# An attention and expert kernel on one core: scores begun half a step sooner, and all ten pairs of query chunks sharing their weights

## The chip, the core and the metric

The kernel runs on one NeuronCore of a Trainium2 chip. PE is the matrix engine (PEld are its weight loads), DVE the vector engine, ACT the scalar engine, POOL the general engine and SP the engine whose queue issues nearly all transfers. The time is the device time of one execution in microseconds (us); lower is better.

## The reference

Two layers one after the other, in fp32: an attention without softmax over 8 sequences of 2496 tokens, and a layer of 8 experts of which each token takes at most one.

```python
scale = 1.0 / S                                  # S = 2496, z: (8, 2496, 64)
scores = scale * np.matmul(z, z.transpose(0, 2, 1))
attn = np.maximum(scores, 0.0) ** 2
x = u * np.matmul(attn, v)                       # u, v: (8, 2496, 256)
x = x.reshape(19968, 256)
do_compute = x @ w_skip > 0
xc = x[do_compute]
e_idx = np.argmax(xc @ w_gate, axis=1)           # and gate_w, its softmax probability
for e in range(8):                               # w1[e]: 256x1024, w2[e]: 1024x256
    h = np.maximum(xc[e_idx == e] @ w1[e], 0.0)
    out[e_idx == e] = xc[e_idx == e] + gate_w[e_idx == e, None] * (h @ w2[e])
```

Queries and keys are the same array z, so the matrix of scores is symmetric, and so are the weights `attn`.

## The kernel before

**Chunks and steps.** A sequence (a batch `b`) is cut into five chunks of queries, c = 0 to 4: four of 512 and the last of 448. A chunk is worked off in ten steps, p = 0 to 9, of 256 keys each; the keys of step p belong to chunk j = p // 2. `ORDER[c]` says in which order chunk c takes its ten steps. There are 8 x 5 x 10 = 400 steps in `steps`. What is called step k below is the place in that order, 0 to 9.

**A step.** `scores` (L280): six matmuls of 64 rows into a PSUM tile `ps` (two buffers). `weights`: ACT makes `r` = relu (L323) and squares it (L324); `r` has five buffers. fp32 is carried as a pair of rounded values: `high` rounds `r` to `ah` (L346, on ACT where `on_act` says so, otherwise on DVE), `low` has DVE make `al` = `r` - `ah` (L350). `ah` and `al` have three buffers each. `attend` (L377): 24 matmuls of 64 rows into the accumulators `acc`, in two halves of 12, d = 0 and d = 1 (the two halves of the features); the step of the last keys has 18. The second half of a chunk's first step is put off into its second, and that of its last but one into its last. A step's scores are issued `LA` = 2 steps ahead: in step k, `stage(s + LA)` issues the scores of step k + 2 on PE, then relu, square, `ah` and `al` are queued on ACT and DVE, and then the 24 matmuls of step k follow.

**Shared weights.** For a pair of chunks (c, j) in `PAIRS`, c < j, the weights that chunk c computes for the keys of chunk j are those that chunk j needs for the keys of chunk c, transposed. `keep` (L297) has DVE turn `r` into a tile `rt` (two buffers, one for a pair of chunks, two transposes a step); two steps later `put_some` issues four transfers `kept<-rt` of 256 KB, in runs of 512 bytes. `ahead` calls `recall` (L311) five steps before the step: one transfer `r<-kept` of 512 KB into a buffer of `r`. A recalled step has no scores, relu or square; in chunk 4 its `ah` and `al` are made in three pieces each. The first batch does not share the pairs of chunk 0. The turning of a chunk's last but one step waits in `put_off`.

**A chunk's end** (`finish`): ACT copies a half of the sums out of PSUM (L405), DVE adds the other (L407), then multiplies by `u` (`mul`, L410), turns the rows (L414), and SP stores them twice (L423) at the ends of steps 3 and 4 of the next chunk. After every second chunk the routing of its tokens follows (`gates`, L445, on PE; small DVE operations L478 to L534). SP's queue is in program order: a transfer that waits for its data or its buffer holds back all behind it. From 1230 us on the experts' part runs (`unit`, L639 to L662).

Of the kernel before, what the change touches and what calls it, by code (L numbers as in the profile page):

```python
# [27 lines left out]

PAIRS = ((0, 1), (0, 2), (0, 3), (1, 2), (1, 3), (2, 3), (2, 4), (3, 4))
ORDER = (
# [22 lines left out]
def attn_moe(ctx, tc, zT, uT, v, wg, w1, w2, cst, pad, out):  # L55
# [183 lines left out]
    def on_act(ci, p):  # L239
        b, c = ci // NQ, ci % NQ  # L240
        j = p // 2
        if (b, c) == (0, 0):
            return p in (4, 6)
        return (j, c) in pairs(b) or (c, j) in pairs(b) or p in EXTRA[c]
# [69 lines left out]
    put_off = []  # L314
# [393 lines left out]
    NP = NB // 2  # L708
    steps = [(ci, p) for ci in range(len(chunks)) for p in order(ci // NQ, ci % NQ)]
    LA = 2  # L710
    NC = len(chunks)
    NZ = SZ // QC
    todo = {}
    aa = {}
# [3 lines left out]

        todo.setdefault(s // 2, []).append(f)

    old, known = {}, set()

    def stage(s):
        if s < len(steps):
            aa[s], high, low = weights(*steps[s], old.pop(s, None), s % NP == NP - 2)
            return high, low
        return lambda: None, lambda: None

    def put_some():

# [5 lines left out]
    def ahead(s):  # L736
        if s < len(steps):
            ci, p = steps[s]
            if (p // 2, ci % NQ) in pairs(ci // NQ):
                old[s] = recall(ci, p)  # L740
                known.add(s)


    def later(s, k, load, *args):
# [5 lines left out]
    for ci, (b, q0, n) in enumerate(chunks):  # L750
# [3 lines left out]
            if chunks[ci + 1][2] == QC:  # L754
                at(s0 + 10, lambda ci=ci: straight(ci + 1))
        if ci == 0:
            first = [(4 * j - 8, j % 2, 3, load_z, j) for j in range(2, NZ)]
            first += [(2 * g - 4, 1, 4, load_v, g) for g in range(2, NB // 2)]
            for s1, _, k, load, j in sorted(first, key=lambda x: x[:2]):
                eng = nc.vector  # L760
                if s1 - k < 0:
                    at(s1, load(0, j, eng))
                else:
                    later(s1 - k, k, load, 0, j, eng)
            at(14, lay_pads)
# [31 lines left out]
    ctx.enter_context(tc.manual_schedule(engines=set(ENGINES)))  # L797

    for s in range(LA):
        for f in stage(s):  # L800
            f()
    accs = {}
    new, left = [], []
    for s, (ci, p) in enumerate(steps):
        b, q0, n = chunks[ci]
        k = s % NP
# [3 lines left out]
            accs[ci] = [[ps_acc.tile([P, QC], F32, name="acc", tag="acc") for _ in range(2)] for _ in range(2)]  # L810
        acc = accs[ci]
        if k < NP - 1:
            high, low = stage(s + LA)
            if k < NP - 2 or s + LA in known:
                high()
                low()
                high = low = lambda: None
            while k == NP - 3 and put_off:
                put_off.pop()()
            attend(b, n, p, 0, acc[0], *aa[s], k == 0, False)  # L820
            for t in () if k in (0, NP - 2) else (s - 1, s) if k == 1 else (s,):
                attend(b, n, steps[t][1], 1, acc[1], *aa.pop(t), t % NP == 0, False)
            rest = high, low
        else:


            part, mul, rows0, rows1, store = finish(ci)
            attend(b, n, p, 0, acc[0], *aa[s], False, True)

            high, low = rest  # L830
            if s + 1 < len(steps) and not on_act(*steps[s + 1]):
                high()
                low()
                high = low = lambda: None
            part(0, 1, acc[0])
            part(0, 0, acc[0])
            high()
            low()
            high, low = stage(s + LA)
            attend(b, n, steps[s - 1][1], 1, acc[1], *aa.pop(s - 1), False, False)  # L840
            if s + LA in known:

                high()
                low()
                high = low = lambda: None
            attend(b, n, p, 1, acc[1], *aa.pop(s), False, True)
            part(1, 1, acc[1])
            high()
            part(1, 0, acc[1])
            low()  # L850
            mul()
            accs.pop(ci)

            new.append(ci)
# [222 lines left out]
```

## Time and profile before

| | before |
|---|---|
| time, median of 3 runs | 1719.31 us (1716.77 to 1723.87) |
| the profiled execution | 1723.13 us, of which 1721.3 us from the first to the last instruction |
| granted clock of PE | 0.996 of full speed over the span |
| PE busy | 98% of the span |
| DVE, ACT, POOL busy | 69%, 67%, 30% |
| moved by DMA | 267 MB |

A busy share is an average over the attention part (about 1230 us) and the experts' part (about 490 us), which have different limits; the chunks of one batch are told apart further down.

### The profile page before, as it was taken

The numbers are of one execution on the slowest core, as the hardware profiler recorded it, in microseconds if no ns is written. First come the engines' busy times: TensorE is split into PE (matmuls) and PEld (weight loads), VectorE is DVE, ScalarE is ACT, GpSimd is POOL, SyncE is SP. The second block draws the span as 40 slices with busy tenths as digits, with TensorE's granted clock in tenths as the row PEclk, the third lists the DMA queues.
The fourth block names the chain that finished last, engine by engine and source line by source line (L and its number), as shares of the span: only waits on it lengthen the run. The fifth ranks groups of instructions, "written<-read, shape, count | busy, mean of one in ns | idle before, by whom it ended". The sixth has DMA issues, their size and how long they took to land.

```text
span 1721.3 us, 39714 instructions
## 1 busy us (share of the span) xinstructions
PE 1679.4 (98%) x15690; PEld 1519.3 (88%) x15690; DVE 1191.2 (69%) x2108; ACT 1151.4 (67%) x1494; POOL 522.7 (30%) x545
## 2 busy tenths in 40 slices
PE   9999999999999999999999999999989999999998
PEld 7889888888988898898889888888889999999998
DVE  7878888887887788788788878877653333333433
ACT  8888887887888888788888877878433323323321
POOL 1103212311320221131123123122344567546631
PEclk9999999999999999999999999999999999999999
DMA  5575688477758847875784787568452244224210
GB/s 197 129 187 156 159 240 229 95 211 226 171 148 215 241 101 200 242 183 145 197 233 112 210 243 192 131 180 219 117 129 64 83 106 113 72 69 108 85 42 31
DMA packets 397964, 267.34 MB, mean 155 GB/s; under 512 B 199920, under 2 KB 328305, under 8 KB 397648
## 3 DMA queue, kind: packets, MB, share of 16 engines
q1 hardware_dynamic: 383584, 240.45, 52.2%
q0 software_dynamic: 13632, 22.99, 4.7%
q8 instruction: 138, 2.26, 0.5%
q14 instruction: 178, 1.46, 0.3%
q10 hardware_dynamic: 432, 0.18, 0.0%
HBM read 145.80 MB, written 118.06 MB: 153 GB/s over the span
## 4 chain that ended last, share of the span: by engine, by line
PE 79%; DVE 6%; ACT 6%; issue 4%; DMA 4%; SPq 0%; POOL 0%; DVEq 0%; ACTq 0%; POOLq 0%
PE acc L377 46%; PE y L662 12%; PE psh L639 11%; PE ps L280 8%; DVE al L350 3%; DMA out<-o,idt 2%; ACT ah L346 2%; ACT r L323 2%; ACT r L324 1%; PE psm L445 1%; DVE rt L297 1%; PE pst L604 1%; DMA kept<-rt 1%; DVE ah L346 1%; DMA r<-kept 0%
## 5 line engine op out<-in xcount | busy, mean ns | idle before, releaser
L377 PE MATMUL acc<-ah,vh 64*128 64x512 f32 (+1 forms) x3120 | 626.6, 373 | 6.1 <-ACT ah L346 3.7
L377 PE MATMUL acc<-ah,vl 64*128 64x512 f32 (+1 forms) x3120 | 611.0, 371 | 0.1
L350 DVE TENSOR_TENSOR al<-r,ah 128x1024 fp32r<-128x1024 f32 (+3 forms) x464 | 488.0, 1068 | 157.3 <-ACT ah L346 132.1
L377 PE MATMUL acc<-al,vh 64*128 64x512 f32 (+1 forms) x3120 | 484.2, 374 | 10.0 <-DVE al L350 8.6
L536 POOL DMA_INDIRECT lst<-pair,dest x160 | 196.5, 1228 | 859.8 <-DVE dest L534 780.7
L377 PEld LDWEIGHTS acc<-ah,vh 64*128 64x128 f32 x3120 | 337.7, 186 | 47.9 <-ACT ah L346 6.7
L323 ACT ACTIVATE r<-ps 128x1024 f32<-128x1024 f32 (+1 forms) x278 | 279.0, 1003 | 146.4 <-PE ps L280 124.6
L377 PEld LDWEIGHTS acc<-ah,vl 64*128 64x128 f32 x3120 | 336.8, 186 | 30.9 <-DVE vl L127 0.5
L377 PEld LDWEIGHTS acc<-al,vh 64*128 64x128 f32 x3120 | 309.0, 186 | 56.2 <-DVE al L350 26.5
L346 ACT CAST ah<-r 128x1024 fp32r<-128x1024 f32 (+3 forms) x381 | 329.2, 889 | 39.4 <-PE acc L377 29.2
L324 ACT ACTIVATE r<-r 128x1024 f32<-128x1024 f32 (+1 forms) x278 | 289.9, 1043 | 8.8
L649 ACT ACTIVATE hh<-psh 128x512 fp32r<-128x512 f32 (+2 forms) x172 | 96.2, 572 | 279.0 <-PE psh L639 200.5
L662 PE MATMUL y<-w2t,hh 128*128 128x256 f32 (+1 forms) x1328 | 233.6, 280 | 2.3 <-ACT hh L649 1.9
L650 DVE SCALAR_TENSOR_TENSOR hl<-psh,hh 128x512 fp32r<-128x512 f32 (+2 forms) x172 | 110.1, 655 | 159.1 <-ACT hh L649 127.2
L662 PEld LDWEIGHTS y<-w2t,hh 128*128 128x128 f32 (+1 forms) x1328 | 204.1, 191 | 4.7 <-ACT hh L649 2.9
L662 PE MATMUL y<-w2t,hl 128*128 128x256 f32 (+1 forms) x664 | 185.1, 279 | 6.3 <-DVE hl L650 3.2
L639 PE MATMUL psh<-xt,w1h 128*128 128x256 f32 (+3 forms) x896 | 176.1, 296 | 1.9 <-issue 1.8
L297 DVE STREAM_TRANSPOSE rt<-r 128x512 f32<-128x512 f32 x244 | 158.3, 687 | 1.7 <-DMA kept<-rt 1.7
L639 PEld LDWEIGHTS psh<-xt,w1h 128*128 128x128 f32 x896 | 140.8, 191 | 4.4 <-issue 2.6
L662 PEld LDWEIGHTS y<-w2t,hl 128*128 128x128 f32 (+1 forms) x664 | 126.8, 191 | 7.9 <-DVE hl L650 4.0
L639 PE MATMUL psh<-xt,w1l 128*128 128x256 f32 (+3 forms) x448 | 132.0, 295 | 1.6 <-issue 1.6
L695 POOL DMA_INDIRECT out<-o,idt x77 | 76.6, 994 | 156.6 <-DVE o L692 123.2
(186 smaller groups left out, 1794.5 us busy)
## 6 DMA issues: line engine op xcount, KB each, us to landing
kept<-rt SPq DMA_DIRECT2D x244, 256.0 KB
r<-kept SPq DMA_DIRECT2D x122, 512.0 KB
raw<-in_v SPq DMA_DIRECT2D x80, 256.0 KB
ut<-in_uT SPq DMA_DIRECT2D x32, 512.0 KB
xr<-xrow SPq DMA_DIRECT2D x128, 128.0 KB
out<-xrow SPq DMA_DIRECT2D x128, 128.0 KB
raw<-in_w SPq DMA_DIRECT2D x64, 256.0 KB
zf<-in_zT SPq DMA_DIRECT2D x40, 256.0 KB
```

Source lines behind the costliest of these rows:

```text
L280: nc.tensor.matmul(to, k[h, o : o + P], queries(ci, q, h, n), start=(m == 0), stop=(m == 2))
L297: nc.vector.transpose(t[:, :, 32 * k : 32 * k + 32].rearrange("p (k a) i -> p a k i", k=4), r[:, x, :].rearrange("p (a k i) -> p a k i", a ...
L323: nc.scalar.activation(r[:, :, :n], ps[:, :, :n], AF.Relu, scale=isc)
L324: nc.scalar.activation(r[:, :, :n], r[:, :, :n], AF.Square)
L346: (nc.scalar.copy if on_act(ci, p) else nc.vector.tensor_copy)(h_, r_)
L350: nc.vector.tensor_sub(l_, r_, f32(h_))
L377: nc.tensor.matmul(acc[t][:, :n], w[h, x, dd], by_halves(a[h, x, :n]), start=(first and t not in halves[:m]), stop=(last and t not in halv ...
L536: put = nc.gpsimd.indirect_dma_start(out=lst, out_offset=bass.IndirectOffsetOnAxis(ap=dest[:, t : t + 1], axis=0), in_=pair[:, t, :], in_o ...
L639: nc.tensor.matmul(ps[:, j * W : (j + 1) * W], wt[:, a, o : o + P], by_halves(x[:, d, :W]) if alt else x[:, d, :W], start=(m == 0), stop=( ...
L649: nc.scalar.activation(oh, by, AF.Relu)
L650: nc.vector.scalar_tensor_tensor(ol, by, 0.0, f32(oh), op0=ALU.max, op1=ALU.subtract)
L662: nc.tensor.matmul(ys[t], h[:, tt], by_halves(w2t[f][:, k, :]), start=(f == 0 and m == 0 and t % share == 0), stop=(f == NF - 1 and m == 2 ...
```

## The change

`PAIRS` becomes all ten pairs (c, j) with c < j, so (0, 4) and (1, 4) are new; the first batch shares six instead of five. Over the 8 batches that is 6 + 7 x 10 = 76 pairs instead of 5 + 7 x 8 = 61, so 30 more steps are recalled, all of them in chunk 4. `ORDER[0]` takes the steps as they come (8 stood between 3 and 4), `ORDER[1]` changes, too. `stage` is split: `begin` issues scores, relu and square, `rounding` queues `ah` and `al`. In step k, `rounding(s + 2)` comes first, then the first half of the step's matmuls, then `begin(s + 3)`, then the second half. The turning of a chunk's last two steps (not only of the last but one) waits in `put_off`, which is now emptied behind the chunk's `mul`. In the first chunk the loads of z are begun two half steps sooner.

```diff
-PAIRS = ((0, 1), (0, 2), (0, 3), (1, 2), (1, 3), (2, 3), (2, 4), (3, 4))
+PAIRS = tuple((i, j) for j in range(5) for i in range(j))
 ORDER = (
-    (0, 1, 2, 3, 8, 4, 5, 6, 7, 9),
-    (2, 3, 0, 4, 1, 5, 8, 6, 7, 9),
+    (0, 1, 2, 3, 4, 5, 6, 7, 8, 9),
+    (2, 3, 0, 4, 5, 1, 6, 7, 8, 9),
     (4, 0, 1, 6, 2, 7, 3, 8, 9, 5),
     (6, 0, 2, 1, 8, 3, 9, 4, 5, 7),
     (0, 1, 2, 3, 4, 5, 6, 7, 8, 9),
...
-    def stage(s):
+    def begin(s):
         if s < len(steps):
-            aa[s], high, low = weights(*steps[s], old.pop(s, None), s % NP == NP - 2)
-            return high, low
-        return lambda: None, lambda: None
+            aa[s], high, low = weights(*steps[s], old.pop(s, None), s % NP >= NP - 2)
+            rounds[s] = high, low
+
+    def rounding(s):
+        for f in rounds.pop(s, ()):
+            f()
...
-            first = [(4 * j - 8, j % 2, 3, load_z, j) for j in range(2, NZ)]
+            first = [(4 * j - 10, j % 2, 3, load_z, j) for j in range(2, NZ)]
...
         if k < NP - 1:
-            high, low = stage(s + LA)
-            if k < NP - 2 or s + LA in known:
-                high()
-                low()
-                high = low = lambda: None
-            while k == NP - 3 and put_off:
-                put_off.pop()()
+            rounding(s + LA)
             attend(b, n, p, 0, acc[0], *aa[s], k == 0, False)
+            if k != 1:
+                begin(s + LA + 1)
             for t in () if k in (0, NP - 2) else (s - 1, s) if k == 1 else (s,):
                 attend(b, n, steps[t][1], 1, acc[1], *aa.pop(t), t % NP == 0, False)
-            rest = high, low
+                if k == 1 and t < s:
+                    begin(s + LA + 1)
         else:
             part, mul, rows0, rows1, store = finish(ci)
             attend(b, n, p, 0, acc[0], *aa[s], False, True)
-            high, low = rest
-            if s + 1 < len(steps) and not on_act(*steps[s + 1]):
-                high()
-                low()
-                high = low = lambda: None
             part(0, 1, acc[0])
             part(0, 0, acc[0])
-            high()
-            low()
-            high, low = stage(s + LA)
             attend(b, n, steps[s - 1][1], 1, acc[1], *aa.pop(s - 1), False, False)
-            if s + LA in known:
-                high()
-                low()
-                high = low = lambda: None
+            rounding(s + LA)
+            begin(s + LA + 1)
             attend(b, n, p, 1, acc[1], *aa.pop(s), False, True)
             part(1, 1, acc[1])
-            high()
             part(1, 0, acc[1])
-            low()
             mul()
+            while put_off:
+                put_off.pop(0)()
             accs.pop(ci)
```

PE's order where two steps of chunk 0 in the middle of the kernel meet, before. `acc_11726` and `acc_11727` take the second half (d = 1) of a step, `acc_11724` and `acc_11725` the first half of the next.

```order
L377 MATMUL acc_11726<-al_11739,vh_10567 128x512
L377 MATMUL acc_11727<-al_11739,vh_10567 128x512
L280 MATMUL ps_11870<-zqh_11551,zh_11289 128x512 x2
L280 MATMUL ps_11870<-zql_11552,zh_11289 128x512 x2
L280 MATMUL ps_11870<-zqh_11551,zl_11290 128x512 x2
L377 MATMUL acc_11724<-ah_11767,vh_10823 128x512
L377 MATMUL acc_11725<-ah_11767,vh_10823 128x512
```

PE's order in the changed kernel at the same place: `acc_11745` and `acc_11746` take the first half of a step, `acc_11747` and `acc_11748` its second.

```order
L377 MATMUL acc_11745<-al_11750,vh_10594 128x512
L377 MATMUL acc_11746<-al_11750,vh_10594 128x512
L280 MATMUL ps_11871<-zqh_11572,zh_11312 128x512 x2
L280 MATMUL ps_11871<-zql_11573,zh_11312 128x512 x2
L280 MATMUL ps_11871<-zqh_11572,zl_11313 128x512 x2
L377 MATMUL acc_11747<-ah_11749,vh_10594 128x512
L377 MATMUL acc_11748<-ah_11749,vh_10594 128x512
```

The six matmuls of the scores have moved from between two steps to between the halves of the step before.

DVE's order at the end of chunk 0, before: the second halves of the sums are added (`xrow`), `al` of a later step, `mul` (`ut`), and the next chunk's first steps.

```order
L407 TENSOR_TENSOR xrow_12173<-acc_11726,xrow_12173 128x512
L350 TENSOR_TENSOR al_12222<-r_12196,ah_12221 128x1024
L410 TENSOR_TENSOR ut_11597<-xrow_12173,ut_11597 128x1024
L534 TENSOR_SCALAR dest_11721<-df_12035 128x2
L350 TENSOR_TENSOR al_12247<-r_12100,ah_12246 128x1024
L350 TENSOR_TENSOR al_12273<-r_12269,ah_12272 128x1024
```

DVE's order in the changed kernel at the same place.

```order
L350 TENSOR_TENSOR al_12225<-r_12197,ah_12224 128x1024
L407 TENSOR_TENSOR xrow_12200<-acc_11747,xrow_12200 128x512
L410 TENSOR_TENSOR ut_11618<-xrow_12200,ut_11618 128x1024
L297 STREAM_TRANSPOSE rt_12240<-r_12035 128x4x4x32 x2
L297 STREAM_TRANSPOSE rt_12240<-r_12106 128x4x4x32 x2
L534 TENSOR_SCALAR dest_11742<-df_12058 128x2
L350 TENSOR_TENSOR al_12263<-r_12123,ah_12262 128x1024
L350 TENSOR_TENSOR al_12289<-r_12285,ah_12288 128x1024
```

Four transposes, those of the new pair (0, 4), stand between `mul` and the next `al`; the `al` ahead of `mul` now stands ahead of the second halves' sum.

SP's order in chunk 3 of a batch in the middle, before. `kept_230` is the pair (3, 4), `kept_229` the pair (2, 4), `raw` a load of v.

```order
L423 DMA xr<-xrow 32x16x64 x4
L423 DMA out<-xrow 32x16x64 x4
L173 DMA ut<-in_uT 128x2x448
L734 DMA kept_230<-rt 32x16x128 x4
L102 DMA raw<-in_v 128x512
L311 DMA r<-kept_229 128x2x512
L110 DMA zf<-in_zT 128x512
```

SP's order in the changed kernel at the same place: `kept_229` is now the pair (0, 4), `kept_230` (1, 4), `kept_231` (2, 4), `kept_232` (3, 4).

```order
L423 DMA xr<-xrow 32x16x64 x4
L423 DMA out<-xrow 32x16x64 x4
L311 DMA r<-kept_229 128x2x512 x2
L173 DMA ut<-in_uT 128x2x448
L739 DMA kept_232<-rt 32x16x128 x4
L311 DMA r<-kept_230 128x2x512 x2
L102 DMA raw<-in_v 128x512
L311 DMA r<-kept_231 128x2x512
L110 DMA zf<-in_zT 128x512
```

Four more recalls, for the first four steps of chunk 4, stand around the write of the pair (3, 4).

## Rows read from the trace of the kernel before

**Rows 1.** The page: the span, and the busy time of each engine with its share of the span.

```profile
span 1721.3 us, 39714 instructions
PE 1679.4 (98%) x15690; PEld 1519.3 (88%) x15690; DVE 1191.2 (69%) x2108; ACT 1151.4 (67%) x1494; POOL 522.7 (30%) x545
```

**Rows 2.** Windows: the five chunks (0 to 4) of the fifth batch, one line each, bounds in us, then length and busy us of each engine, the granted clock, the share of the 16 DMA engines' time, GB/s.

```profile
624.30:655.40 31.10, 31.10 (x291) 27.29 (x289) 25.28 (x32) 28.77 (x29) 10.18 (x12) 1.00 0.55 136
655.40:687.60 32.20, 31.92 (x316) 26.55 (x315) 26.76 (x56) 26.55 (x31) 3.72 (x3) 1.00 0.69 181
687.60:717.50 29.90, 29.38 (x272) 25.75 (x268) 21.70 (x28) 24.28 (x28) 8.27 (x9) 1.00 0.87 243
717.50:749.70 32.20, 31.20 (x306) 26.13 (x308) 26.43 (x52) 22.75 (x28) 5.13 (x4) 1.00 0.80 212
749.70:775.60 25.90, 25.90 (x272) 25.60 (x270) 22.86 (x36) 21.52 (x35) 9.00 (x12) 1.00 0.63 172
```

**Rows 3.** The chain that ended last, in order of time (start us, length us, what). The first two rows stand at the same place of chunk 4 in the third and in the fifth batch; those behind them are a step with 448 queries, one with 512, and the routing's matmuls.

```profile
446.41 12.48 PE acc L377 x132
751.62 12.48 PE acc L377 x132
...
764.72 2.27 PE acc L377 x24
766.99 0.60 PE ps L280 x6
...
818.89 2.59 PE acc L377 x24
821.48 0.65 PE ps L280 x6
845.44 1.01 PE psm L445 x32
```

**Rows 4.** Waits over the whole span: engine and line, what ended the wait, us in total, times, longest us.

```profile
ACT r L323 <- PE ps L280: 124.6, 107, 4.3
DVE al L350 <- ACT ah L346: 132.1, 130, 3.2
PEld acc L377 <- DVE al L350: 26.5, 46, 1.2
PE acc L377 <- DVE al L350: 8.6, 18, 0.8
PEld acc L377 <- ACT ah L346: 6.7, 8, 1.2
```

**Rows 5.** Lines by form: the operations of DVE and then of ACT in a chunk 4 (901.2 to 929.5 us); after the bar busy us, mean ns of one.

```profile
L350 DVE TENSOR_TENSOR al<-r,ah 128x896 fp32r<-128x896 f32 x5 | 5.5, 1092 | 1.1 <-ACT ah L346 0.6
L350 DVE TENSOR_TENSOR al<-r,ah 128x384 fp32r<-128x384 f32 x8 | 4.0, 541 | 0.0
L350 DVE TENSOR_TENSOR al<-r,ah 128x128 fp32r<-128x128 f32 x4 | 1.1, 285 | 0.0
L346 DVE CAST ah<-r 128x896 fp32r<-128x896 f32 x3 | 2.0, 673 | 0.0
...
L324 ACT ACTIVATE r<-r 128x896 f32<-128x896 f32 x4 | 3.8, 952 | 0.1
L323 ACT ACTIVATE r<-ps 128x896 f32<-128x896 f32 x4 | 3.7, 915 | 0.5 <-PE ps L280 0.5
L346 ACT CAST ah<-r 128x384 fp32r<-128x384 f32 x8 | 3.7, 509 | 2.5 <-PE acc L377 2.0 <-ACT vh L126 0.5
L346 ACT CAST ah<-r 128x128 fp32r<-128x128 f32 x4 | 1.2, 293 | 0.0
```

**Rows 6.** Timelines of the fifth batch's chunk 0 (it begins at 624.3): ACT's and DVE's rows of steps near its middle, and SP's row that writes the first pair (start us, length us, engine, line, operation, in brackets the idle time before and what ended it).

```profile
640.71 1.02 ACT L323 ACTIVATE r<-ps 128x1024 f32<-128x1024 f32 x1
641.76 1.07 ACT L324 ACTIVATE r<-r 128x1024 f32<-128x1024 f32 x1
642.86 1.05 ACT L346 CAST ah<-r 128x1024 fp32r<-128x1024 f32 x1
...
643.94 1.23 DVE L350 TENSOR_TENSOR al<-r,ah 128x1024 fp32r<-128x1024 f32 x1 [0.79 <-ACT ah L346]
645.83 1.31 DVE L297 STREAM_TRANSPOSE rt<-r 128x512 f32<-128x512 f32 x2 [0.66 <-DMA kept<-rt]
...
638.10 3.90 SPq L734 DMA_DIRECT2D kept<-rt  x4
```

**Rows 7.** Timelines around the start of the fifth batch's chunk 3 (717.5): the copy, the sum and `mul` at the end of chunk 2.

```profile
718.32 0.58 ACT L405 COPY xrow<-acc 128x512 f32<-128x512 f32 x1
...
719.79 0.69 DVE L407 TENSOR_TENSOR xrow<-acc,xrow 128x512 f32<-128x512 f32 x1
720.51 1.23 DVE L410 TENSOR_TENSOR ut<-xrow,ut 128x1024 f32<-128x1024 f32 x1
```

**Rows 8.** The same chunk 3: SP's timeline, and the transfers' rate in 40 equal slices of the window 717.5 to 749.7 (0.8 us each), GB/s.

```profile
731.56 2.23 SPq L423 DMA_DIRECT2D xr<-xrow  x4
733.83 2.76 SPq L423 DMA_DIRECT2D out<-xrow  x4
739.08 3.71 SPq L734 DMA_DIRECT2D kept<-rt  x4
...
GB/s 345 233 284 233 187 106 324 361 349 369 389 410 402 255 8 0 0 0 68 152 153 217 187 201 215 144 149 376 182 176 168 233 246 205 221 229 155 237 158 163
```

More of the change, by code (lines that the diff above doesn't have):

```diff
@@ L719, in at @@
         todo.setdefault(s // 2, []).append(f)
-    old, known = {}, set()
-    def stage(s):
+    old, soon = {}, []
+    rounds = {}
+    def begin(s):
         if s < len(steps):
-            aa[s], high, low = weights(*steps[s], old.pop(s, None), s % NP == NP - 2)
-            return high, low
-        return lambda: None, lambda: None
+            aa[s], high, low = weights(*steps[s], old.pop(s, None), s % NP >= NP - 2)
[3 more added lines that the diff above has]
+            f()
     def put_some():
@@ L740, in ahead @@
                 old[s] = recall(ci, p)
-                known.add(s)
     def later(s, k, load, *args):
@@ L760, in attn_moe @@
                 eng = nc.vector
-                if s1 - k < 0:
+                if s1 < 0:
+                    soon.append(load(0, j, eng))
+                elif s1 - k < 0:
                     at(s1, load(0, j, eng))
@@ L799, in attn_moe @@
     for s in range(LA):
-        for f in stage(s):
-            f()
+        begin(s)
+        rounding(s)
+    for f in soon:
+        f()
+    begin(LA)
     accs = {}
```

## The prediction

> **What bounds the kernel now.** I read the page first: PE is busy for 98% of the span [rows 1]. The change touches only the attention part, so next come the windows of the five chunks of one batch: PE is busy for 149.5 of 151.3 us, DVE for 123.0, ACT for 123.9 (sums of the columns), and the transfers' share runs from 0.55 in chunk 0 to 0.87 in chunk 2 [rows 2]. A busy PE may still be a waiting one, so the chain gives its pace. A step's 24 matmuls take 2.59 us with 512 queries and 2.27 us with 448 [rows 3]: the ratio, 0.876, is that of the columns (0.875), so the matmuls stream without gaps. The Trainium skill (Perfetto Trace Analysis, section Identifying the Most-Contended Engine) says that matmul busy time tells little of the headroom and that weight loads' busy share should be taken. By that measure chunk 0, with 27.3 of 31.1 us, would have 12% to spare, and fewer matmuls would buy little; the pace speaks against it, but it is one of the rivals.
>
> From the pace follows a floor. Two batches are 751.62 - 446.41 = 305.2 us apart [rows 3], 152.6 us a batch. A chunk has 9 x 24 + 18 = 234 matmuls: four chunks of 512 take 4 x 234 x 2.59 / 24 = 101.0 us, the one of 448 takes 234 x 2.27 / 24 = 22.1. Of 50 steps 16 are recalled; 28 scores of 0.65 and 6 of 0.61 make 21.9, the routing's matmuls 2.5 x 1.0. That is 147.5 us: PE loses about 5.1 us a batch, 41 us in all, to waits. The waits view names them: the matmuls and weight loads of `acc` wait for `al` of DVE (26.5 + 8.6 us) and for `ah` of ACT (6.7). Behind that lies ACT, which waits 124.6 us for scores, and DVE, which waits 132.1 us for ACT [rows 4]. So the stretch is bound by PE's columns, with a chain scores, relu, square, `ah`, `al` that is now and then a little late.
>
> **The change part by part.**
>
> *Scores that go away.* 30 steps in chunk 4, six matmuls each, 0.60 to 0.62 us a step [rows 3]: 30 x 0.61 = 18.3 us less on PE. If PE is the bound, all of it is gained.
>
> *What they cost elsewhere.* ACT loses 30 x (0.915 + 0.952) = 56 us; 30 roundings move from DVE to ACT, 15 in the new pairs' own chunks at 1.05 us [rows 6], 15 in chunk 4 in three pieces, 2 x 0.51 + 0.29 = 1.31 us [rows 5], and 15 more that ACT has already become three pieces: 35 to 40 us come back. DVE gains 60 transposes at 0.65 (39 us) and 30 x (2 x 0.541 + 0.285 - 1.092) = 8 us of pieces, and loses 30 roundings of 0.67 (20 us): +27 us, 3.5 a batch, where it has 28 us idle [rows 2, 5, 6]. Both lie beside PE's work and cost nothing by themselves. The thin place is chunk 4: there DVE is busy 22.9 of 25.9 us [rows 2], and PE's work shrinks by 2.4 us. DVE's cover there is down to about 1 us; its neighbours, chunks 3 and 0, have 6 us each.
>
> *Scores half a step sooner.* The chain from the first score to `al` is 0.65 + 1.02 + 1.07 + 1.05 + 1.23 = 5.0 us [rows 3, 6]; it has two steps of 3.24 us, that is 1.5 us of slack, which one foreign operation on ACT or DVE eats. The second half of a step, 12 matmuls or 1.30 us, moves behind the scores, and `ah` now stands ahead of the next relu on ACT instead of behind it. Slack becomes 2.8 us or more. At a chunk's start the gain is larger, since before the rounding of the next chunk's first steps stood behind ACT's copies of the sums. Nothing in the trace shows a longer lead. The bounds are none of the 41 us and all of it; I take a bit under half, 18 us, because the waits are short (a mean of 0.6 us [rows 4]) but some are of DVE's own queue, which no earlier score helps.
>
> *Turning behind the sums.* This adds waits, at the end of chunks 0 and 1 (two steps, 2 x 1.31 us of transposes) and 2 (one). Behind them on DVE stands `al` of the next chunk's third step. From the chunk's last matmul: copy 0.58, sum 0.69, `mul` 1.23, transposes 2.6, `al` 1.23, together 6.3 us [rows 6, 7]. PE reaches the use of that `al` after 1.30 + 0.65 + 3.89 + 0.65 us and eight matmuls on `ah`, 0.86: 7.35 us. One us is left. The turned `r` also hold two of five buffers until then: counting allocations, the fourth step's `r` takes one of them, so its relu can start at 5.1 us, and 1.02 + 1.07 + 1.05 + 1.23 later, at 9.5, its `al` is there, needed at about 10. Half a us is left. I take 0.5 us a batch, 4 us; the bounds are 0 and 6.5 us a batch (all transposes uncovered), 52 us.
>
> *The natural order in chunk 0.* Step 8 no longer stands between the first two pairs, so the third pair's turning comes one step sooner. It needs the first pair's `rt` tile, and in some batches it already waits 0.66 us for the transfer that empties it, until 645.83 [rows 6]. One step sooner it would wait 0.66 + 3.24 = 3.9 us, and the next `al` comes at 645.8 + 1.3 + 1.23 = 648.3, where PE needs it at 624.3 + 1.95 + 4.55 + 5 x 3.24 + 0.86 = 647.9. So 0.4 us late, in 7 batches: 3 us; bounds 0 and 27 us (all 3.9).
>
> *More transfers.* 15 pairs: 15 x 1.05 MB written and read. The place is chunk 3: it asks for 8 recalls instead of 4, five of them for chunk 4, in steps 5 to 9. The row of rates shows runs of reads at 324 to 410 GB/s (372 on average over the seven slices) and stretches of writes around 200 [rows 8]. Reads of 6.0 MB at 372 and writes of 3.15 MB at 200 are 16.0 + 15.7 = 31.7 us in a chunk that will last some 29: 3 us spill into chunk 4, whose own share is only 0.63 [rows 2]. The stores now begin 14.1 us into the chunk [rows 8]. From there in SP's order: stores 5.2, two recalls 2.8, u 1.2, the pair (3, 4) 5.2, six recalls and six loads 12.7, and 1.5 us to settle: the last recall is there at 42.7 us. It is rounded for step 7 of chunk 4, which begins at 29 + 1.1 + 3.4 + 5 x 2.27 = 44.9, less 1.5: 43.4. Hidden, by 0.7 us. I take 0.5 us a batch, 4 us; bounds 0 and 24 (3 us late in each batch). The Trainium skill (DMA: Bandwidth & Descriptors, section Specifications) gives about 358 GB/s of HBM per core and lets runs of 512 bytes go at full rate. By that, chunk 3's 9.1 MB take 25.5 us, nothing spills, and the 4 us are 0; the rows differ on both counts, since reads went above it and the 512-byte writes stayed far below.
>
> The start (one `zh` of 0.6 us ahead of the third relu) and the experts' part change nothing.
>
> **Sum.** -18.3 - 18 + 4 + 3 + 4 = -25.3 us. The profiled execution took 1723.13 us, 3.8 above the median of the runs; -25.3 from that median gives 1694 us.
>
> **The rivals.**
>
> *The waits only move.* The columns go, but the new waits eat what the longer lead gives: 1719.3 - 18.3 = 1701 us. For it: the margins above are all under 1 us. Against it: ACT, the busiest beside PE in chunk 0 (28.8 of 31.1 us), gets more lead.
>
> *No new waits, or fewer old ones.* Without the 11 us of new waits the sum is 1683 us; with all old ones gone as well 1719.3 - 18.3 - 41 = 1660. The near end is likelier, since DVE's own queue stays as full as it is.
>
> *Columns are not the bound* (this is what the rule on weight loads would make of it; on this kernel's rows it would come through DVE, which fills chunk 4). Then the 18.3 us are not gained; the longer lead (18) less the new waits (11) leaves 7: 1712 us. For it: DVE's 1 us of cover there. Against it: the 6 us on either side.
>
> *Slower.* The deferred transposes stand ahead of `al` and hold the buffers of `r`. If DVE comes to a chunk's end more than 1 us behind, every us of them shows, at worst 6.5 us in each of 7 to 8 batches, 49 us: 1719.3 - 18.3 - 18 + 49 = 1732 us. It makes the kernel slower than before from 36 / 7.5 = 4.8 us a batch on. Against it: DVE idles 5 to 8 us in each of chunks 0 to 3 [rows 2], so it seldom comes late to their ends.
>
> **How the numbers follow.** 0.5 for the forecast, 0.22 for the waits that only move, 0.1 for fewer waits, 0.1 for DVE as the bound, 0.08 for slower. A measurement of this kernel tells about 0.5% (8.6 us) from no change. Faster by more: the first three, 0.82, less a little of the second case's tail: 0.8; within: 0.12; slower: 0.08. The range from 1680 to 1712 takes in the bounds down to no new waits at all; it leaves out the far end of fewer waits (0.04), half of DVE as the bound (0.05) and the slow case.
>
> **What would show it.** In the chain, chunk 4 with two groups of scores instead of six, and two batches 299 us apart instead of 305.2. ACT's wait for `ps` well under 124.6 us. A wait of DVE's transposes (`rt`) for `kept<-rt` of 2 to 4 us in chunk 0, without PE waiting behind it. In chunk 3 a transfer share above 0.9 and in chunk 4 no wait of `ah` for `r<-kept`. I would be wrong if `acc` waited for `ah` in chunk 4 with `r<-kept` behind it, or for `al` in the third and fourth steps of chunks 1, 2 and 3.

## The result and the profile after

The changed kernel is slower: 1732.27 us, median of five runs (1731.24 to 1739.07), beside 1720.74 us for the kernel before on the same chip; ratio 1.0073, 95% interval 1.0046 to 1.0100. The forecast was 1694 us, with a range from 1680 to 1712. The profiled execution took 1731.65 us.

The page of the kernel after begins so (to be read against [rows 1]):

```profile
span 1729.9 us, 39688 instructions
PE 1671.4 (97%) x15510; PEld 1524.7 (88%) x15510; DVE 1213.5 (70%) x2198; ACT 1127.5 (65%) x1524; POOL 518.8 (30%) x545
```

PE has 180 matmuls fewer and is busy for 8 us less, but the span has grown by 8.6 us. Its windows show the chunks of the fifth batch, columns as in [rows 2]:

```profile
623.70:656.40 32.70, 31.54 (x290) 27.47 (x289) 23.91 (x32) 29.47 (x31) 10.47 (x13) 1.00 0.52 124
656.40:688.00 31.60, 31.60 (x314) 26.93 (x313) 29.00 (x61) 27.22 (x31) 5.00 (x4) 1.00 0.83 217
688.00:717.30 29.30, 29.30 (x274) 25.55 (x271) 24.10 (x30) 24.42 (x27) 7.41 (x9) 1.00 0.98 248
717.30:745.90 28.60, 28.60 (x292) 25.26 (x291) 26.83 (x57) 20.48 (x29) 5.43 (x4) 1.00 0.95 278
745.90:775.50 29.60, 27.23 (x268) 26.32 (x265) 22.62 (x40) 19.20 (x35) 7.13 (x12) 0.94 0.80 227
```

Chunks 2 and 3 run without a gap, with the DMA engines' share at 0.98 and 0.95. Chunk 4, the one that lost scores, grew from 25.9 to 29.6 us: PE idles there for 2.4 us, and its mean clock is 0.94. (The bounds are the first matmuls of each chunk, and scores of the next chunk move across them, so a single length says little.)

The waits over the whole span, to be read against [rows 4]:

```profile
ACT ah L346 <- DMA r<-kept: 103.0, 73, 7.1
DVE al L350 <- ACT ah L346: 87.2, 102, 5.3
ACT r L323 <- PE ps L280: 77.2, 92, 3.0
DVE rt L297 <- DMA kept<-rt: 28.0, 7, 6.2
PEld acc L377 <- DVE al L350: 21.2, 28, 2.3
PEld acc L377 <- ACT ah L346: 17.8, 7, 3.8
PE acc L377 <- ACT ah L346: 15.5, 6, 3.5
PE acc L377 <- DVE al L350: 11.8, 17, 2.0
```

The waits that the longer lead was to shorten are shorter: ACT for scores 124.6 to 77.2, DVE for `ah` 132.1 to 87.2. New is ACT's wait for recalled tiles, 103.0 us, and behind it PE's wait for `ah`, 6.7 to 17.8 on the weight loads and 15.5 on the matmuls. The chain around the start of the fifth batch's chunk 4, columns as in [rows 3], shows it as the bound, with `acc` behind `ah` behind `r<-kept`, which the prediction had named as a sign of being wrong:

```profile
737.39 6.72 PE acc L377 x64
744.11 7.58 DMA r<-kept
...
751.76 1.13 ACT ah L346 x3
752.89 0.04 issue
752.94 9.90 PE acc L377 x84
762.84 0.62 PE ps L280 x6
763.45 2.27 PE acc L377 x24
```

A recall issued at 744.11 releases ACT 7.58 us later, and PE starts again at 752.94. The 84 matmuls behind take 9.90 us, where 84 at the pace of 2.27 for 24 take 7.95: another 2 us. The windows right behind the wait (the number ahead of the last two is the granted clock) tell why:

```profile
752.90:754.00 1.10, 1.06 (x12) 1.06 (x14) 0.87 (x3) 0.78 (x2) 0.00 (x0) 1.00 1.06 406
754.00:757.50 3.50, 3.50 (x22) 3.20 (x20) 3.13 (x9) 2.09 (x7) 1.85 (x2) 0.51 1.06 386
757.50:762.00 4.50, 4.50 (x50) 4.50 (x50) 4.50 (x6) 2.75 (x8) 3.35 (x9) 1.00 1.04 367
```

About 1.1 us after PE has started again the clock falls to its lower level, 1.2 GHz, for 3.4 us. The Trainium skill (TensorE: Matmul & The Clock Gate, section HAM oscillation — how this bites in real kernels) describes a wait for a transfer after which the next tile starts on the slow clock; the trace agrees in part. Three such spells, 13.7 us in all, lie in the attention part of the profiled run, and none in that of before. They belong to waits of 2.5, 3.6 and 3.0 us in the chunks 4 of the fifth, seventh and eighth batch, and in the last two the fall came 0.4 and 0.8 us before PE started again; behind waits of 3.3 and 2.2 us in that of the third batch the clock stayed up. So not every long wait has such a spell behind it.

To compare kernels by stage I use PE's *lost time*: how much later matmuls start than the pace of their columns allows (24 in 2.27 or 2.59 us), worked out from all matmuls of a trace; it holds waits and half-speed spells alike. Mean of the second to eighth batch, us per batch:

| kernel | chunk 0 | 1 | 2 | 3 | 4 | sum |
|---|---|---|---|---|---|---|
| before | 0.30 | 0.84 | 0.44 | 1.82 | 0.62 | 4.0 |
| after | 1.19 | 0.46 | 0.14 | 0.03 | 4.72 | 6.5 |
| sched8 | 0.06 | 0.33 | 0.12 | 0.00 | 0.10 | 0.6 |
| nowrite | 1.20 | 0.46 | 0.14 | 0.34 | 4.82 | 7.0 |
| noread | 1.22 | 0.46 | 0.14 | 0.72 | 0.82 | 3.4 |
| nine14 | 1.33 | 0.35 | 0.14 | 0.00 | 0.96 | 2.8 |
| own_first | 2.71 | 0.46 | 0.14 | 0.49 | 2.04 | 5.8 |
| actq | 1.15 | 0.46 | 1.46 | 0.42 | 4.24 | 7.7 |
| loads_early | 1.50 | 0.76 | 1.07 | 0.18 | 4.27 | 7.8 |
| stores_late | 1.21 | 0.46 | 0.14 | 0.91 | 0.83 | 3.6 |
| stores_both | 0.01 | 0.33 | 0.14 | 0.51 | 0.63 | 1.6 |
| both_last8 | 0.01 | 0.28 | 0.13 | 0.45 | 0.13 | 1.0 |
| pairs10 | 2.87 | 1.70 | 2.52 | 1.91 | 2.61 | 11.6 |
| pairs10b | 6.11 | 4.05 | 0.98 | 1.03 | 2.21 | 14.4 |

Over the whole attention part the lost time is 38.7 us before and 58.2 after: +19.5, against the 18.3 us of scores that went. That part ends 2.6 us later after than before (1234.9 and 1232.3); the other 6 us of the 8.6 lie in the experts' part behind it.

SP's timeline of the fifth batch's chunk 3 (717.3 to 745.9), to be read against [rows 8], shows how the recall got late:

```profile
729.48 3.58 SPq L423 DMA_DIRECT2D xr<-xrow  x4
733.11 3.78 SPq L423 DMA_DIRECT2D out<-xrow  x4
736.99 1.42 SPq L311 DMA_DIRECT2D r<-kept  x2
738.50 0.76 SPq L173 DMA_DIRECT2D ut<-in_uT  x1
739.34 4.66 SPq L739 DMA_DIRECT2D kept<-rt  x4
744.11 2.71 SPq L311 DMA_DIRECT2D r<-kept  x2
...
753.56 0.36 SPq L311 DMA_DIRECT2D r<-kept  x1
```

From 729 on one row follows the other: issuing the four transfers of a store or of a pair takes SP 3.6 to 4.7 us, while the engines' share is 1.02 (729.4 to 737) and 0.95 (737 to 744). The shortest issue of one such transfer of a pair in this run took 0.30 us, which points to the engines as what holds SP here. The recalls for the third and fourth steps of chunk 4 stand behind 1 MB of stores, two recalls, `u` and the pair (3, 4).

### The profile page after: what moved, and what is told of

Its sections match the earlier page's. It is cut to its first block, busy times and chain, and to the rows that moved or that the text cites. A ratio compares the mean times of both kernels' runs of the same rounds, so it can differ in the third digit from the quotient of the medians.

```text
span 1729.9 us, 39688 instructions
## 1 busy us (share of the span) xinstructions
PE 1671.4 (97%) x15510; PEld 1524.7 (88%) x15510; DVE 1213.5 (70%) x2198; ACT 1127.5 (65%) x1524; POOL 518.8 (30%) x545
## 4 chain that ended last, share of the span: by engine, by line
PE 77%; DMA 10%; DVE 6%; issue 3%; SPq 2%; ACT 1%; POOL 0%; another core or an unknown queue 0%; DVEq 0%; POOLq 0%; ACTq 0%
PE acc L377 45%; PE y L662 11%; PE psh L639 11%; PE ps L280 8%; DMA r<-kept 4%; DVE al L350 3%; DMA out<-o,idt 2%; DMA kept<-rt 1%; PE pst L604 1%; DVE rt L297 1%; PE psm L445 1%; DMA xr<-xrow 1%; SPq L739 1%; DMA raw<-in_v 1%; SPq L423 0%
## 5 line engine op out<-in xcount | busy, mean ns | idle before, releaser
L377 PE MATMUL acc<-ah,vh 64*128 64x512 f32 (+1 forms) x3120 | 667.5, 377 | 18.7 <-ACT ah L346 15.5
L377 PE MATMUL acc<-ah,vl 64*128 64x512 f32 (+1 forms) x3120 | 649.1, 373 | 0.0
L350 DVE TENSOR_TENSOR al<-r,ah 128x1024 fp32r<-128x1024 f32 (+2 forms) x524 | 489.5, 959 | 107.7 <-ACT ah L346 87.2
L377 PE MATMUL acc<-al,vh 64*128 64x512 f32 (+1 forms) x3120 | 515.4, 374 | 12.0 <-DVE al L350 11.8
L346 ACT CAST ah<-r 128x1024 fp32r<-128x1024 f32 (+2 forms) x471 | 367.9, 806 | 145.9 <-DMA r<-kept 103.0
L377 PEld LDWEIGHTS acc<-ah,vh 64*128 64x128 f32 x3120 | 385.6, 187 | 61.4 <-ACT ah L346 17.8
L377 PEld LDWEIGHTS acc<-ah,vl 64*128 64x128 f32 x3120 | 384.5, 187 | 28.4 <-DVE vl L127 0.4
L377 PEld LDWEIGHTS acc<-al,vh 64*128 64x128 f32 x3120 | 340.3, 187 | 49.6 <-DVE al L350 21.0
L323 ACT ACTIVATE r<-ps 128x1024 f32<-128x1024 f32 (+1 forms) x248 | 251.5, 1014 | 83.2 <-PE ps L280 77.2
L324 ACT ACTIVATE r<-r 128x1024 f32<-128x1024 f32 (+1 forms) x248 | 261.0, 1052 | 7.9
L297 DVE STREAM_TRANSPOSE rt<-r 128x512 f32<-128x512 f32 x304 | 195.4, 684 | 28.0 <-DMA kept<-rt 28.0
```

The costliest lines, as they stand in the source:

```text
L297: nc.vector.transpose(t[:, :, 32 * k : 32 * k + 32].rearrange("p (k a) i -> p a k i", k=4), r[:, x, :].rearrange("p (a k i) -> p a k i", a ...
L323: nc.scalar.activation(r[:, :, :n], ps[:, :, :n], AF.Relu, scale=isc)
L324: nc.scalar.activation(r[:, :, :n], r[:, :, :n], AF.Square)
L346: (nc.scalar.copy if on_act(ci, p) else nc.vector.tensor_copy)(h_, r_)
L350: nc.vector.tensor_sub(l_, r_, f32(h_))
L377: nc.tensor.matmul(acc[t][:, :n], w[h, x, dd], by_halves(a[h, x, :n]), start=(first and t not in halves[:m]), stop=(last and t not in halv ...
```

## The experiments

The kernel before took 1705 to 1706 us beside the first and the last four kernels and 1721 to 1724 beside the others, so kernels are compared by their ratio to it alone. The difference seems to lie in the experts' part: in single profiled runs it takes 468 to 474 us in the first and the last four kernels, 486 to 496 in all others. The code of that part is the same in all.

**sched8: the new order of issue without the two pairs.**

```
-PAIRS = tuple((i, j) for j in range(5) for i in range(j))
+PAIRS = ((0, 1), (0, 2), (0, 3), (1, 2), (1, 3), (2, 3), (2, 4), (3, 4))   # and ORDER as before
```

> The changed kernel with the eight pairs and the step orders of before: scores half a step sooner, rounding and turning as in the change. Theory A (the two new pairs' transfers fill the DMA engines in chunks 2 and 3, and the recalls of chunk 4 come late; the new order of issue itself helps): PE's waits in chunk 4 fall from 4.7 us to under 1, those of chunks 1 to 3 stay as low as in the changed kernel (0.6 us together, 3.1 before); 1700 to 1710 us, ratio to before 0.988 to 0.994. Theory B (turning behind the sums and the held r buffers make the kernel late, in chunk 4 too): no gain of waits and 18 us more of scores than the changed kernel, 1740 to 1750 us, ratio 1.01 or more.

Ratio 0.986 (0.9845 to 0.9875), run again as sched8_again 0.9843 (0.9826 to 0.986). Two lines of the page:

```profile
span 1677.8 us, 39768 instructions
L346 ACT CAST ah<-r 128x1024 fp32r<-128x1024 f32 (+3 forms) x381 | 332.7, 889 | 65.5 <-PE acc L377 40.1
```

Its windows, chunks 3 and 4 of the fifth batch:

```profile
705.30:735.70 30.40, 30.40 (x308) 26.95 (x307) 27.37 (x54) 23.13 (x29) 6.23 (x4) 1.00 0.89 248
735.70:761.60 25.90, 25.90 (x272) 25.59 (x272) 22.21 (x36) 20.56 (x33) 10.56 (x12) 1.00 0.63 168
```

PE fills both windows, and `ah` waits for PE's buffers rather than for recalls. The new order alone takes nearly all lost time away, 4.0 to 0.6 us a batch, more than theory A asked for; theory B has fallen.

**pairs10 and pairs10b: the two pairs without the new order.**

```
-PAIRS = ((0, 1), (0, 2), (0, 3), (1, 2), (1, 3), (2, 3), (2, 4), (3, 4))
+PAIRS = tuple((i, j) for j in range(5) for i in range(j))                  # and ORDER as after
-            aa[s], high, low = weights(*steps[s], old.pop(s, None), s % NP == NP - 2)
+            aa[s], high, low = weights(*steps[s], old.pop(s, None), s % NP == NP - 2 and steps[s][1] < 8)   # pairs10b only
```

> The kernel before with all ten pairs and the changed kernel's step orders, everything else as before. Theory A: the waits of chunk 4 are there as in the changed kernel (4 us or more a batch, ah behind r<-kept), and the waits of chunks 1 to 3 of before (3.1 us a batch) come on top; 18 us of scores are gone: 1719 - 18 + 8 x 4.1 = 1734 us, ratio 1.005 to 1.012. Theory B: without the new order the columns are simply gained, 1701 us, ratio 0.99.

> The kernel before with ten pairs and the changed step orders, and the last block's pairs turned at their rounding (in the earlier run without the new order of issue their turning was put off past that of their second half, which mixed their data and held a buffer of r for eight steps; that run told too much at once). Volume theory: chunk 4 waits 3 us or more a batch for r<-kept as in the changed kernel, and the waits of chunks 1 to 3 of before stay: 18 us of scores less, 24 to 33 us of waits more, ratio 1.003 to 1.010. If the pairs cost nothing without the new order: 0.99.

Ratios 1.0235 (1.0217 to 1.0252) and 1.0373 (1.0342 to 1.0403). Chunk 4 waits for recalls here too (2.2 to 2.6 us), but that is the smaller part, which neither expectation had. The waits of pairs10b:

```profile
PEld acc L377 <- DVE al L350: 93.9, 82, 4.5
PE acc L377 <- DVE al L350: 63.2, 50, 4.1
DVE rt L297 <- DMA kept<-rt: 52.3, 17, 5.9
```

Turned at their rounding, the last block's pairs stand on DVE ahead of the sums of chunks 0 and 1, behind a wait for `rt`, and PE loses 6 and 4 us there. So with the old order of issue the turning ahead of the sums is dear, where I had taken the turning behind them for a cost; no run has the new order of issue with the turning ahead of the sums.

**nowrite and noread: one direction of the new transfers alone.**

```
-            for a in range(4):
+            for a in range(0 if b > 1 and j == 4 and c < 2 else 4):              # nowrite
                 puts.append((step[0], dst[:, :, a * P : a * P + P], t[32 * a : 32 * a + 32]))
-        nc.sync.dma_start(r, src[...])
+        if ci // NQ > 1 and ci % NQ == 4 and p < 4: nc.gpsimd.memset(r, 0.5)     # noread
+        else: nc.sync.dma_start(r, src[...])
```

> The changed kernel without the transfers that write the pairs (0,4) and (1,4), from the third batch on (what is recalled is stale; the turning stays). These writes lie in chunks 0 and 1. Theory A (chunks 2 and 3 are full): DVE's 28 us of waiting in chunk 0 for kept<-rt shrink, but chunk 4 still waits 3 us or more a batch for r<-kept; 1720 to 1730 us. If the writes carry the cost: waits of chunk 4 under 1.5 us, below 1710 us.

> The changed kernel with the recalls of (0,4) and (1,4) replaced by a GpSimd memset of the same buffer, from the third batch on (the written pairs are never read). Theory A: the waits of chunk 4 fall to under 1 us a batch in these six batches, 1732 - 6 x 4.5 = about 1703 us, and the half-speed spells of the clock in chunk 4 go. If not the recalls but what DVE or ACT do at the chunk's end makes chunk 4 late: no change, 1728 to 1735 us.

nowrite 1.0061 (1.0045 to 1.0076), noread 0.9857 (0.9835 to 0.9879). Without the writes chunk 4 loses 4.8 us as before; without the recalls the same two windows of the fifth batch read:

```profile
711.00:739.80 28.80, 28.62 (x287) 24.73 (x289) 26.86 (x57) 19.63 (x28) 6.82 (x6) 1.00 0.90 242
739.80:765.50 25.70, 25.64 (x268) 25.01 (x267) 22.21 (x40) 18.83 (x35) 10.05 (x15) 1.00 0.76 204
```

Chunk 4 is full again, and there are no half-speed spells in the attention part. The lateness hangs on the recalls. DVE's waits for `rt` stayed at 27 us in nowrite, so the writes of the fourth pair in chunk 0 do not make them.

**nine14: one pair fewer.**

```
+PAIRS = tuple((i, j) for j in range(5) for i in range(j) if (i, j) != (0, 4))
```

> The changed kernel without the pair (0,4): nine pairs, 8 of 16 new transfers fewer, chunk 4 begins with two scores of its own. If the DMA engines' volume in chunks 2 and 3 is what makes the recalls late, two recalls (3.4 us of all engines) fewer stand between the 4 to 5 us of lateness and none: waits of chunk 4 about 1 to 1.5 us a batch, and 8 us of scores are gained on the eight-pair version: ratio to before 0.985 to 0.99. If each recalled pair of chunk 4 costs its own wait, half of the waits stay (2.4 us): 0.993 to 0.997.

0.9873 (0.9853 to 0.9893). Four fifths of chunk 4's lost time go with half of the new recalls: a queue that has just become too full, not a price per recall.

**own_first: chunk 4 begins with its own two scores.**

```
-    (0, 1, 2, 3, 4, 5, 6, 7, 8, 9),
+    (8, 9, 0, 1, 2, 3, 4, 5, 6, 7),      # ORDER[4]; the six loads of chunk 4 two steps later
```

> The changed kernel with chunk 4 in the order 8, 9, 0 to 7 (its two own scores first; the loads of chunk 4 shifted by two steps, as their buffers come free two steps later). Each recall is still issued five steps ahead of its use, so it is issued 5 us later too, out of the full chunk 3 into chunk 4, where the engines have a fifth of their time free. If the full stretch is the cause: waits of chunk 4 fall from 4.7 us a batch to 1 to 2, ratio to before 0.985 to 0.992. If the lead of five steps (five buffers of r) is what is short, the waits stay at 4 us or more, ratio 1.003 to 1.008.

0.9951 (0.9936 to 0.9966). Chunk 4's loss falls to 2.0 us as expected, but chunk 0's rises to 2.7, and with it the expected time is missed. In the fifth batch the last recalled tiles are rounded at the very end of chunk 4, ahead of ACT's copies of its sums, and PE's weight loads wait 1.5 us for such a copy at the next chunk's start: the lateness has moved to where the sums leave.

**actq: recalls in a queue of their own.**

```
-        nc.sync.dma_start(r, src[...])
+        nc.scalar.dma_start(r, src[...])
```

> The changed kernel with all recalls issued by ScalarE's DMA queue instead of SyncE's; same volume. If the recalls are late because they stand in one queue behind writes, stores and loads that fill it: waits of chunk 4 under 1.5 us, ratio 0.985 to 0.99. If the engines' volume itself is the limit, somebody is late all the same (the writes hold rt, and DVE's turning waits; or raw and z come late): ratio 0.998 to 1.008. ScalarE could lose time where a recall waits for its buffer.

1.0038 (1.0019 to 1.0056). Its windows, chunks 3 and 4 of the fifth batch:

```profile
726.70:755.30 28.60, 28.60 (x290) 25.29 (x289) 26.70 (x57) 20.04 (x28) 5.45 (x4) 1.00 0.99 300
755.30:784.20 28.90, 26.54 (x266) 24.48 (x263) 20.63 (x39) 18.59 (x35) 8.61 (x13) 1.00 0.76 197
```

Two lines of its waits:

```profile
ACT ah L346 <- DMA raw<-in_v: 28.4, 4, 9.0
ACT ah L346 <- DMA r<-kept: 23.8, 10, 6.1
```

The share in chunk 3 goes to 0.99, ACT's wait for recalls from 103.0 to 23.8, and others come late instead: loads of v, for which ACT now waits 28.4 us, and the lost time of chunk 4 hardly moves. That fits the Trainium skill (DMA: Bandwidth & Descriptors, section Issuing engines are not separate DMA queues): the queues of both engines drain through the same 16. It is the engines that are full, not SP's queue.

**loads_early: seven loads moved out of chunks 2 and 3.**

```
-            jobs = [(load_v, 0, 1, 3), (load_z, 0, 1, 6), (load_v, 1, 2, 3), (load_z, 1, 2, 5), (load_v, 2, 2, 7)]
-            jobs += [(load_v, 3, 3, 3), (load_v, 4, 3, 4), (load_v, 5, 3, 6), (load_v, 6, 3, 7)]
+            jobs = [(load_v, 0, 0, 5), (load_z, 0, 0, 7), (load_v, 1, 0, 9), (load_z, 1, 1, 1), (load_v, 2, 1, 3)]
+            jobs += [(load_v, 3, 1, 5), (load_v, 4, 1, 7), (load_v, 5, 1, 9), (load_v, 6, 2, 1)]
```

> The changed kernel with the next batch's loads of v 0 to 6 and z 0 and 1 moved one to two chunks forward, out of chunks 2 and 3 into chunks 0 and 1: seven transfers of 256 KB, each 0.85 us of all engines by the packets' times, 2.5 us out of chunk 2 and 3.4 out of chunk 3. If volume is the cause: waits of chunk 4 fall by about that, from 4.7 to 1 to 2 us a batch; against it up to 1 us a batch in chunk 0, where ScalarE is busy for 0.9 of the time: ratio 0.985 to 0.995. If not: 1.005 or more.

1.0030 (1.0013 to 1.0047). A miss for plain volume: chunk 4 gained 0.5 us a batch, and chunks 0 to 2 lost 1.5, where the loads now stand. Chunk 3 of the fifth batch has room now, and chunk 4 waits all the same:

```profile
723.50:752.60 29.10, 28.97 (x290) 24.78 (x288) 24.12 (x52) 19.33 (x25) 4.72 (x4) 1.00 0.83 227
752.60:781.00 28.40, 25.85 (x266) 24.88 (x266) 22.97 (x40) 19.17 (x35) 7.08 (x12) 1.00 0.83 242
```

The loads left the first half of chunk 3; the recalls are late from its second half on. Volume of a chunk is the wrong measure. What counts may be what stands in the queue between the stores and the recalls; the next runs test that.

**stores_late, stores_both, nine_stores: the stores moved.**

```
                 for f, k in after:
+                    if f is store and ci % NQ == 2 and b + 1 < B: k += 13      # all three: chunk 2's, into chunk 4
+                    if f is store and ci % NQ == 4: k += 5                     # stores_both: chunk 4's, later in chunk 0
                     todo.setdefault(s + k, []).append(f)
```

> The changed kernel with the stores of chunk 2's rows (1 MB) issued in steps 6 and 7 of chunk 4, behind the last recall, instead of steps 3 and 4 of chunk 3, in all batches but the last; nothing else. The order of SyncE's queue is otherwise the same and the volume too. Theory W (SyncE's queue is full from the stores in the middle of chunk 3 to the last recall in chunk 4; what counts is what stands between them, and the loads at the chunk's start do not): the recalls land about 3.5 to 4 us earlier and the waits of chunk 4 fall from 4.7 to 1 to 1.5 us a batch; 7 x 3.5 = 25 us less, ratio to before 0.990 to 0.995. If the lead of five buffers of r is what is short: no change, 1.005 or more.

> The same late stores with nine pairs, without (0,4). Theory W: nine pairs wait 1.0 us a batch in chunk 4 and 1.3 in chunk 0; the first goes: 1 us a batch, ratio 0.981 to 0.985 where nine pairs alone had 0.987. If the stores have nothing to do with it: 0.987.

> As the late stores, and the stores of chunk 4's rows as well: steps 8 and 9 of the next chunk 0 instead of 3 and 4, behind the writes of the first three pairs. There the stores stand between two pairs' writes, and DVE's turning waits 28 us in all for kept<-rt. Theory W: these waits go and with them up to 1 us a batch of PE's 1.2 us in chunk 0: 0.005 below the late stores of chunk 2 alone. If chunk 0's waits come from the two rt tiles alone: the same as that kernel.

stores_late 0.9902 (0.988 to 0.9924): with the same transfers, 1.7 points under the changed kernel, where 25 us (1.5) had been expected. SP's timeline of its chunk 3 (709.7 to 739.0):

```profile
722.89 1.18 SPq L311 DMA_DIRECT2D r<-kept  x2
724.17 0.86 SPq L173 DMA_DIRECT2D ut<-in_uT  x1
729.42 3.67 SPq L739 DMA_DIRECT2D kept<-rt  x4
733.19 2.18 SPq L311 DMA_DIRECT2D r<-kept  x2
```

Its windows, the same chunk 3 and chunk 4:

```profile
709.70:739.00 29.30, 29.17 (x292) 25.06 (x292) 26.77 (x57) 20.88 (x29) 5.06 (x4) 1.00 0.88 277
739.00:764.60 25.60, 25.60 (x268) 24.90 (x265) 21.66 (x40) 19.12 (x35) 8.00 (x13) 1.00 0.92 251
```

The recall for chunk 4's third step is issued 23.5 us after chunk 3's start instead of 26.8. Ahead of the pair (3, 4) SP issues nothing from 725.0 to 729.4, and the engines work off what stands in the queue (share 1.02, 382 GB/s); PE fills chunk 4. nine_stores had 0.988 (0.9859 to 0.99), a miss: chunk 4's loss went from 0.96 to 0.25 as expected, but the time did not follow within the interval. stores_both had 0.9866 (0.9845 to 0.9886): chunk 0's lost time is gone, 1.21 to 0.01, and DVE waits for `kept<-rt` for 3.0 us in all, where it waited 29.8 in stores_late. SP's rows of the changed kernel, in chunk 0 of the fifth batch, show a store between the writes of two pairs:

```profile
637.83 3.95 SPq L739 DMA_DIRECT2D kept<-rt  x4
641.82 4.11 SPq L423 DMA_DIRECT2D out<-xrow  x4
646.03 3.66 SPq L739 DMA_DIRECT2D kept<-rt  x4
```

So the stores between two pairs' writes made most of the wait for `rt`.

**after_last8, both_last8, sched8_both: the last batch, and late stores without the pairs.**

```
     def pairs(b):
+        if b == B - 1: return [x for x in PAIRS if x[1] < 4 or x[0] > 1]    # the two *_last8
```

sched8_both is sched8 with the stores of stores_both, both_last8 is stores_both with the line above.

> The changed kernel with the eight pairs of before in the last batch alone, ten in the others. If the experts' part is longer because the last batch's recalls come late and PE's wait there sets off half-speed spells of its clock: 6.8 us of waits in the last chunk, 3 of clock there, and the 6 us behind it go, less 2.3 us of scores: ratio to before 0.998 to 1.001 instead of 1.007. If only the waits of that chunk go: 1.003 to 1.005.

> Ten pairs with the stores of chunks 2 and 4 late (ratio 0.987 before), and the eight pairs in the last batch, where the late stores of chunk 2 could not be had. The last chunk there waited 4.3 us. Its waits go, 2.3 us of scores come back: ratio 0.985; with 10 us of half-speed spells behind the attention gone as well 0.980.

> Eight pairs with the new order of issue and the stores of chunks 2 and 4 late. With eight pairs PE waits 0.6 us a batch, so if the place of the stores matters only where the queue is full: the same as eight pairs alone, within 0.002. If late stores help in themselves: 0.005 less.

> Eight pairs with the new order of issue once more, beside the three others: ratio 0.986 as before; both_last8 should be 0.001 to 0.006 below it if the columns of the two new pairs (16 us in seven batches) are worth more than what is left of their waits.

after_last8: 1.0049 (1.0032 to 1.0066), which is what only the last chunk's waits would give, but the interval overlaps that of the changed kernel. sched8_both: 0.9845 (0.9832 to 0.9859), no different from sched8_again; with eight pairs the place of the stores is worth nothing that shows. both_last8: 0.9812 (0.9795 to 0.9828), the best of all: its slowest run (1677.15 us) lies under the fastest of sched8_again (1678.46), though the two intervals touch. One line of its page:

```profile
L299 DVE STREAM_TRANSPOSE rt<-r 128x512 f32<-128x512 f32 x296 | 190.5, 685 | 2.3 <-DMA kept<-rt 2.3
```

The turning of the two pairs waits 2.3 us in all, beside 28.0 in the changed kernel.

## Why the prediction was wrong

**What bounds the kernel** was right: PE's columns, with waits of some us a batch. Where the waits are mostly gone, fewer columns show as time. both_last8 has 156 matmuls of scores fewer than sched8_both, 26 steps or 15.9 us, and some 3 us more of lost time; its attention part ends at 1196.4 us instead of 1206.7. So "columns are not the bound" is out.

**Scores half a step sooner** was too small: 18 us forecast; the new order with eight pairs lost 14.4 us in the attention part instead of 38.7, that is 24.3, and 1.4 to 1.6% of the time is 24 to 27 us. Half of the old waits were expected to stay, some of them as waits in DVE's own queue. sched8 changes the order of that queue, too, so the 24.3 us are those of the whole new order; what the earlier scores give by themselves no run shows.

**Turning behind the sums**, 4 us forecast, costs nothing that shows: chunks 1 to 3 of the changed kernel, where it would, lose 0.46, 0.14 and 0.03 us, less than before. So the slower rival, which rested on it, did not come. The kernel did get slower, to which the prediction gave 0.08, but by another way, and that the chance was there is luck. pairs10b fits the other side (6 us lost in chunk 0 with the turning ahead of the sums), though it has the old order of issue as well.

**The natural order in chunk 0**: the wait of DVE for `rt` was foreseen (3.9 us in each of 7 batches; 7 waits make 28.0), and PE's lost time there rose by 0.9 us a batch, where 0.4 had been put. The forecast looked at the order of pairs; stores_both shows what it left out, the stores that stand in SP's queue ahead of a pair's write: without them there the loss is 0.01 us. Set against sched8, whose gain is taken in full above, it is 1.1 us a batch, 8 us in the seven batches.

**More transfers** is the step that failed: 4 us forecast, bounds 0 and 24. Against sched8, chunk 4's lost time is 4.6 us a batch higher in the second to eighth batch and 0.7 in the first, some 33 us, outside the bounds. The sum of the queue was near: the third recall was put at 28.5 us from the chunk's start (the sum of what stands ahead of it) and issued at 26.8. That is partly luck, since the stores began 12.2 us into the chunk instead of 14.1, but took 7.5 us instead of 5.2. Two things were wrong. I tested only the last recall ("hidden by 0.7 us"); the first to be late is the third, behind the pair (3, 4). And I gave it 1.4 us and "1.5 us to settle", where 7.58 us pass from its issue until ACT is released (4.9 to 10.6 us for the recalls that stand in the chain of the other batches from the third on): SP's rows show when a transfer enters the engines' backlog, not when it leaves. At 26.8 + 7.6 = 34.4 us it is 2.4 us behind the 32.0 that follow from the forecast's own step times (29 + 1.1 + 3.4 us, less 1.5). What came on top was not in the sum at all: the three half-speed spells, 2 us lost in the fifth batch and some 6 in all.

**The rule on bandwidth** that the prediction cites would have made this term 0, further off than the rows were: it counts a chunk's bytes, and the trace has a backlog at one place in it.

In sum: -18.3 for columns, -24.3 for the new order, +8 in chunk 0 and +33 in chunk 4 make -1.6; the attention part ended 2.6 us later, so some 4 us lie in none of these terms. The 6 us in the experts' part stay open. Three more half-speed spells there (10.2 us, about 5 lost) are part of it. Among the kernels beside which the kernel before took 1720 us or more, the experts' part of single profiled runs takes 486 to 496 us in no order that the change explains; the last batch's recalls were tried as the cause (after_last8) and not confirmed. In nowrite, where chunk 4 is as late, no such spell lies in that part (474.3 us).

## What to carry to other kernels

When a change adds transfers, write down the queue in its order from the last moment when it was empty, and test each transfer that something waits for, the first ones behind the big writes above all, with the time from issue to release that the trace shows under load. Work that is not urgent (stores) may cost nothing until the queue is full, and then moving it a few steps can be worth about as much as dropping the transfers it delays (0.9866 with both stores moved, 0.986 without the two pairs). An optimization that saves PE's columns paid here only together with room in the queue that feeds it: beside the same order without them, the two pairs cost about 2% with the stores where they were and gave 0.3% once those had moved and the last batch was left out.

## What the runs showed of the hardware

A wait of PE of a few us can cost more than itself: 3.4 us at half the clock behind it, 2 us more in the case shown. It need not: of five waits from 2.2 to 3.6 us in the chunks 4 of the changed kernel, three had such a spell and two, one of them of 3.3 us, had none. A second queue moved more in the full stretch (300 GB/s in chunk 3 against 278), but only changed who was late. In the changed kernel's chunk 3 the four transfers of a pair (256 KB each, runs of 512 bytes) held SP for 4.66 us and the four of a store (128 KB each) for 3.6 to 3.8, with the engines' share at 0.95 to 1.02; so SP's own timeline showed the full queue from 729.5 us on, where PE waits from 750.2 on.
